# Tap gradients of a depthwise convolution: from TensorE products to GpSimd products and sums

## The chip, the core and the metric

The kernel runs on one core of a Trainium2 chip. The core has TensorE (PE: matrix products; the profile shows its weight loads as PEld), VectorE (DVE), ScalarE (ACT), GpSimd (POOL) and SyncE (SP, which here only starts DMAs). Each engine works through its own list of instructions in order and waits on semaphores for the others. SBUF is the on-chip memory, PSUM the small memory that TensorE writes its products to; GpSimd works on SBUF only in this kernel. The metric is the device time of one execution in microseconds. Times of before and after are medians of several executions; the profile is one further execution with its own time.

## The reference

The kernel computes the output and all gradients of one branchformer block, for x of 2 x 4000 x 144 in bfloat16. What matters here is the gated branch and its convolution over time:

```python
h = _gelu(jnp.einsum('btd,de->bte', xc, w_mlp_in))
u, g = (h[..., :D].copy(), h[..., D:].copy())
g = _layernorm(g, axis=-1)
gp = jnp.pad(g, ((0, 0), (pad, pad), (0, 0)))
gc = jnp.zeros_like(g)
for i in range(K):
    gc = gc + gp[:, i:i + T, :] * dw_csgu[i][None, None, :]
loc = jnp.einsum('btd,de->bte', u * gc, w_mlp_out)
```

The other branch is softmax attention over the 4000 positions. The reference takes the vector-Jacobian product of the whole block. The gradient of the five taps, `dw_csgu` (5 x 144), is for tap i and channel c the sum over batch and time of g(t + i - 2, c) x dgc(t, c), where dgc is the gradient that arrives at gc. Nothing in it couples two channels.

## The kernel before

The two batches are handled one after the other. The 4000 positions of a batch lie as 32 blocks of 125: partition p holds positions 32p to 32p + 31, and block j is the j-th of each partition. So a shift by one position is a shift by one block, and only the ends need a neighbour's partition.

`phase_att` loops over query tiles t = 0 to 32. In a step it forms the scores of tile t and the score gradients of tile t - 1 in four "quads" of products (`quad`, L1028 and L1034) into two PSUM buffers `ps`. VectorE (`S_min` L1052, `PdP` L1070) and ScalarE (L1073) take them out; ScalarE takes exponentials (`P_exp`, L1060); VectorE multiplies in SBUF (L1075). DMA transposes issued by SP turn the results (L1064 for a whole tile, L1255 for half a tile), and TensorE multiplies them again: `Y_half` L1084, `Z_half` L1130, and the gradient of x in `X_group` L1175, which VectorE adds up at L1181. GpSimd scales rows for the X products (L1108 to L1112) and copies remainders into `qz` (L1003), from which SP transposes the next query tile `qt` (L1010).

The gated branch is cut into small functions, `units`, spread over the same loop: 16 rounds per batch, each with two blocks (G2 = 2), about two query tiles per round. `z_unit` to `e_gp` make the forward part of round n, `gc_unit` to `e_dh` the gradient of round o, two rounds behind, `t_unit` transposes. In a ring of five tiles, `gd`, each round leaves its normalized g (index 0) and dgc (index 1); two more such tiles hold the shifted ends.

The tap gradients are made by `dwc_unit`, called after every second round in two parts. Part 0 takes for four blocks and four taps the 128 x 128 matrix of g (shifted) against dgc, summed over positions by TensorE (L668); part 1 takes the fifth tap (L670) and the last 16 channels of all taps (L671). Only the diagonals of these matrices are wanted. `flush` copies each result by ScalarE into the SBUF buffer `l_fl` (L650), and GpSimd adds it to the accumulator `A_dwc` (L651). `dwi_unit` does the same for another weight gradient, with L683, and shares `flush` and `l_fl`. At the end `Final.dwc` picks the diagonals out by six masked products of VectorE (L1677, L1678), transposes them on TensorE and stores `out5` in six DMAs.

The order in which every engine's instructions stand is written out: the table `ORDER` holds, for each engine, the numbers of the instruction groups in the order to be issued, made beforehand by a planner outside the kernel, and `Planner.plan` imposes it. Whenever a group is added or taken away, the whole table has to be made again. WARM is the number of products on zeros that TensorE does at the start, while the first inputs arrive.

Of the kernel before, what the change touches and what calls it, by code (L numbers as in the profile page):

```python
# [15 lines left out]
D = 144  # L16
# [454 lines left out]
WARM = 110  # L471
# [5 lines left out]
def local_units(k, W, b, S, A, es, DHT, ps_w):  # L477
# [5 lines left out]
    sm = es.enter_context(tc.tile_pool(name="loc_sm%d" % b, bufs=4, side="right", reuse_waits="tile"))  # L483
# [20 lines left out]
    fl = pl.tile([128, 512], F32, name="l_fl")  # L504
# [151 lines left out]
    def gnb(h):  # L656
        return gd(h // G2)[:, 0, h % G2, 0:128]

    def dwc_unit(g, part):
        pw = ps_w.tile([128, 512], F32, tag="w")  # L660
        bl = blocks(g)
        for n_, (gg, bi) in enumerate(bl):
            i = G2 * gg + bi
            first, last = n_ == 0, n_ == len(bl) - 1
            t = gd(gg + 1)
            if part == 0:
                for kk in range(4):
                    nc.tensor.matmul(pw[:, kk * 128:(kk + 1) * 128], gnb(i + kk), t[:, 1, bi, 0:128], start=(first and kk == 0), stop=last, skip_group_check=True)  # L668
            else:
                nc.tensor.matmul(pw[:, 0:128], gnb(i + 4), t[:, 1, bi, 0:128], start=first, stop=last, skip_group_check=True)  # L670
                nc.tensor.matmul(pw[0:80, 128:128 + D], rem[:, 0, i:i + 5, :].rearrange("p a b -> p (a b)"), t[:, 1, bi, :], start=False, stop=last, skip_group_check=True)  # L671
        if part == 0:
            flush(pw[:], 128, A.dwc[:, 0:512])
        else:
            flush(pw[:, 0:128], 128, A.dwc[:, 512:640])
            flush(pw[0:80, 128:128 + D], 80, A.dwc[0:80, 640:784])
# [12 lines left out]
    def add(f, *a):  # L689
        def u():  # L690
            f(*a)
        u.tag = f.__name__[:6] + (str(a[-1]) if f.__name__ in ("z_unit", "dwc_unit") else "")
        units.append(u)

    def round_(n, o, c):

        new = [(z_unit, n, 0), (z_unit, n, 1), (e_tanh, n), (e_h, n), (e_stats, n), (dug_unit, n), (e_gn, n), (e_dgc, n), (e_m, n), (e_gp, n)]
        old = [(gc_unit, o), (e_du, o), (dgn_unit, o), (e_dh, o)]
        end = [(dhT_unit, o)]
        if o is not None and o % 2:  # L700
            end += [(dwc_unit, o, 0), (dwc_unit, o, 1), (dwi_unit, o)]
        tr = [(t_unit, c, c - 2 if c is not None and c >= 2 else None)]
        if n is None:
            new = [None] * 10
        if o is None:
            old, end = [None] * 4, [None]
        if c is None:
            tr = [None]
        for u_ in (new[0:3] + old[0:1] + new[3:5] + old[1:2] + new[5:7] + old[2:3] + new[7:9] + old[3:4] + new[9:10] + tr + end):
            if u_ is not None:  # L710
                add(*u_)
# [12 lines left out]
for _s in """  # L724
PE 10 1 1 1 1 1 1 1 1 1 1 1 1 1 1 1 1 1 1 1 1 1 1 1 1 1 167 3 -169 1 1 1 1 1 1 1 1 1 1 162 2 11 -174 1 1 1 1 1 1 1 1 1 1 1 1 1 1 1 1 1 1 179 2 -180 1
# [1316 lines left out]
```

## Time and profile before

| what | us |
|---|---|
| three timed executions | 1278.3, 1276.53, 1277.78 |
| median | 1277.78 |
| the profiled execution, its own time | 1280.24 |
| its span on the core | 1278.4 |
| mean granted TensorE clock | 0.994 |

The span is cut by engine into busy time; a share is of the span. The loop of the first batch fills the span from about 50 to 565 us, that of the second from about 663 to 1183. The stretch between holds the end of the first batch and the start of the second, and the last 95 us the final products. In lists of groups a row gives the line of the kernel, the engine, the operation, what it writes and reads with its shape, how often it stands, its busy time in us, the mean of one in ns, and behind the second bar the idle time of that engine just before it, with what ended it. In the timeline a row gives start and length in us. Durations of TensorE products overlap, because they are pipelined; what one costs in a row of equal ones is the distance between starts.

### The profile page before, as it was taken

What the parts mean: (1) busy time and instruction counts of PE and PEld (TensorE: products, weight loads), DVE (VectorE), ACT (ScalarE), POOL (GpSimd) and SP (SyncE); (2) the same over time, 40 slices, a digit from 0 to 9 for tenths busy, and PEclk for the clock granted to TensorE, in tenths of its full rate; (3) what the DMA queues carried; (4) which work ended last, traced back from release to release, by engine and by line L of the source; (5) the groups of instructions that cost most, each with busy time, mean ns of one, the idle gap of its engine ahead of it and who ended that gap; (6) DMA issues with size and microseconds to landing.
All of it is one profiled execution on the core that took longest, in us unless ns stands there. A gap on an engine that the chain in (4) does not pass through costs nothing.

```text
span 1278.4 us, 38874 instructions
## 1 busy us (share of the span) xinstructions
PE 1251.6 (98%) x15838; PEld 1040.0 (81%) x15838; DVE 1050.6 (82%) x2825; ACT 760.2 (59%) x1232; POOL 477.5 (37%) x971
## 2 busy tenths in 40 slices
PE   8999999999999999999998999999999999999997
PEld 7778888887888888899887788888878788888996
DVE  7699898988888987879768888888889898977765
ACT  4966666656656665545745666665655666555373
POOL 7643443333433443213623434433334333333020
PEclk9999999999999999999999999999999999999999
DMA  3699899798889888885248898888889888899722
GB/s 104 135 165 153 148 147 166 143 158 143 147 158 155 146 157 150 150 191 152 82 99 159 153 160 155 154 156 154 139 159 155 146 154 145 162 148 172 190 60 67
DMA packets 630206, 186.52 MB, mean 146 GB/s; under 512 B 612336, under 2 KB 624971, under 8 KB 630021
## 3 DMA queue, kind: packets, MB, share of 16 engines
q1 hardware_dynamic: 629271, 183.57, 78.9%
q8 instruction: 124, 2.03, 0.6%
q14 instruction: 55, 0.45, 0.1%
q0 software_dynamic: 208, 0.25, 0.1%
q10 hardware_dynamic: 548, 0.21, 0.1%
HBM read 20.82 MB, written 14.22 MB: 27 GB/s over the span
## 4 chain that ended last, share of the span: by engine, by line
PE 87%; DVE 6%; DMA 3%; POOL 1%; ACT 1%; issue 1%; SPq 0%; POOLq 0%; ACTq 0%; DVEq 0%
PE X L1175 21%; PE ps L1028 15%; PE yz L1130 10%; PE yz L1084 9%; PE ps L1034 7%; PE Hps L1458 4%; PE po L1555 3%; PE pc L608 1%; PE pj L991 1%; DVE Pb L1052 1%; DMA SX<-SX 1%; PE pd L556 1%; PE pd L623 1%; PE pw L668 1%; PE pw L683 1%
## 5 line engine op out<-in xcount | busy, mean ns | idle before, releaser
L1052 DVE TENSOR_SCALAR_CACHE_REDUCE Pb<-ps 125x1000 bf16<-125x1000 f32 x256 | 306.0, 1196 | 82.8 <-PE ps L1034 80.1
L1060 ACT ACTIVATE Pb<-Pb,nm 125x1000 bf16<-125x1000 bf16 x256 | 278.7, 1127 | 110.4 <-DVE nm L1054 104.2
L1175 PE MATMUL X<-SX 125*125 125x144 bf16 x2048 | 297.2, 229 | 2.2 <-ACT l_fl L650 0.7
L1175 PE MATMUL X<-SX,Pb 125*125 125x144 bf16 x2048 | 292.7, 226 | 0.0
L1175 PEld LDWEIGHTS <-SX 125*125 125x125 bf16 x2048 | 259.6, 137 | 25.9 <-issue 24.9
L1073 ACT CAST SX<-ps 125x1000 bf16<-125x1000 f32 x189 | 188.1, 995 | 153.4 <-PE ps L1034 151.5
L1028 PE MATMUL ps<-xaT_m,qt 128*125 128x500 bf16 x1024 | 260.8, 375 | 3.8 <-DVE Pb L1052 3.4
L1175 PEld LDWEIGHTS <-Pb 125*125 125x125 bf16 x2048 | 260.5, 137 | 3.2 <-issue 2.5
L1181 DVE TENSOR_TENSOR acc<-X,acc 125x432 f32<-125x432 f32 x372 | 199.9, 548 | 32.0 <-PE X L1175 30.1
L1028 PEld LDWEIGHTS <-qt 128*125 128x125 bf16 x1024 | 122.1, 137 | 44.0 <-issue 5.5
L1130 PE MATMUL yz<-xa_aug,SX 125*125 125x144 bf16 x2048 | 152.4, 229 | 4.2 <-ACT ty L1100 2.8
L1130 PEld LDWEIGHTS <-SX 125*125 125x125 bf16 x2048 | 140.6, 138 | 11.2 <-issue 8.9
L1084 PE MATMUL yz<-xa_aug,SX 125*125 125x145 bf16 x2048 | 146.8, 227 | 0.1
L1084 PEld LDWEIGHTS <-SX 125*125 125x125 bf16 x2048 | 137.1, 137 | 2.0 <-issue 1.6
L1075 DVE TENSOR_TENSOR SX<-SX,Pb 125x1024 bf16<-125x1024 bf16 x189 | 131.2, 698 | 7.3 <-ACT SX L1073 5.6
L1034 PEld LDWEIGHTS <-qt 16*125 16x125 bf16 x1024 | 36.5, 128 | 99.5 <-issue 99.5
L1034 PE MATMUL ps<-XR,qt 16*125 16x500 bf16 x1016 | 111.7, 420 | 0.0
L1070 DVE TENSOR_TENSOR SX<-ps,Pb 125x1000 bf16<-125x1000 f32 x67 | 79.9, 1192 | 8.0 <-ACT SX L1073 5.2
L651 POOL TENSOR_TENSOR A_dwc<-l_fl,A_dwc 128x512 f32<-128x512 f32 (+2 forms) x48 | 36.6, 762 | 82.2 <-ACT l_fl L650 82.2
L633 POOL TENSOR_SCALAR l_w<-gd,nc,c 125x144 f32<-125x144 bf16 x64 | 29.1, 460 | 90.6 <-DVE c L631 81.7
L526 POOL TENSOR_SCALAR l_a<-l_sq 125x576 bf16<-125x576 bf16 x32 | 23.1, 723 | 94.1 <-ACT l_sq L524 93.7
L1110 POOL TENSOR_SCALAR g<-qz,rl 125x144 f32<-125x144 bf16 x62 | 26.1, 421 | 84.0 <-DVE rl L1090 83.7
(479 smaller groups left out, 2327.4 us busy)
## 6 DMA issues: line engine op xcount, KB each, us to landing
go_h<-in_grad_out_dram SPq DMA_DIRECT2D x4, 567.0 KB
Yg<-ug_d SPq DMA_DIRECT2D x4, 567.0 KB
Yn_d<-yn SPq DMA_DIRECT2D x64, 35.2 KB
Zn_d<-qz SPq DMA_DIRECT2D x64, 35.2 KB
ug_d<-ugr SPq DMA_DIRECT2D x32, 70.3 KB
SX<-in_x_dram SPq DMA_DIRECT2D x16, 140.6 KB
out_dram<-Pb SPq DMA_DIRECT2D x16, 140.6 KB
out_dram<-SX SPq DMA_DIRECT2D x16, 140.6 KB
```

Source lines behind the costliest of these rows:

```text
L1028: mm = nc.tensor.matmul(pp[r // 2][:, r % 2, 0:CH], QT[i][:, 3 * h, 0:PB], xaTm[:, c * CH:(c + 1) * CH], start=True, stop=False)
L1034: nc.tensor.matmul(pp[r // 2][:, r % 2, 0:CH], QT[i][rs, 1 + h, 0:PB], xr, start=False, stop=True)
L1052: nc.vector.tensor_scalar(pv(Pbuf, i % NPB, c2), src, -1.0, 3.0e38, op0=ALU.mult, op1=ALU.min, accum_out=NM[i][:, c2:c2 + 1])
L1060: nc.scalar.activation(v, v, ACT.Exp, bias=NM[i][:, 4:5], scale=-1.0)
L1070: nc.vector.tensor_tensor(pv(Sbuf, i % NDB, c2), src, pv(Pbuf, i % NPB, c2), op=ALU.mult)
L1073: nc.scalar.copy(pv(Sbuf, i % NDB, c2), src)
L1075: nc.vector.tensor_tensor(sc, sc, pchunk(i % NPB, c2), op=ALU.mult)
L1084: nc.tensor.matmul(Y, PT[0:PB, j, 0:PB], xaa[:, j, 0:D + 1], start=(j == 0), stop=(j == NB - 1))
L1130: nc.tensor.matmul(Z, ST[0:PB, j, 0:PB], xaa[:, j, 0:D], start=(j == 0), stop=(j == NB - 1))
L1175: nc.tensor.matmul(X[:, jj, :], l, r, start=(n_ == 0), stop=(n_ == len(ops) - 1))
L1181: nc.vector.tensor_tensor(av, X[:, 0:nj, :], av, op=ALU.add)
L1458: nc.tensor.matmul(H[a // 6][0:rows, a // 3 % 2, (a % 3) * D:(a % 3 + 1) * D], lhs, self.src[h][:, 2 + j, :], start=(j == 0 and a % 3 == 0 ...
```

## The change

The tap gradients no longer go through TensorE. `dwc_unit` now runs after every round and gives GpSimd, for each of the round's two blocks, five products of g (shifted by the tap) and dgc, 125 x 144 each, from bfloat16 into a float32 buffer `l_pr` of 125 x 5 x 144, and one sum of that buffer into the accumulator `A_dwc`, now 125 x 5 x 144. The sum over the 125 partitions is left for the end: `Final.dwc` splits the accumulator into a high and a low bfloat16 part on VectorE and multiplies a column of ones with both on TensorE; the result is stored with one DMA. The flush buffer `fl` of `dwi_unit` is now the front of `l_pr`. To make room, the pool `loc_sm` of small tiles has three buffers instead of four. WARM goes from 110 to 116. The order table is made anew for all five engines, with issue times of SP's DMAs that were taken from a trace; `dwi_unit` now stands before `dwc_unit`.

```diff
-WARM = 110
+WARM = 116
...
-    sm = es.enter_context(tc.tile_pool(name="loc_sm%d" % b, bufs=4, side="right", reuse_waits="tile"))
+    sm = es.enter_context(tc.tile_pool(name="loc_sm%d" % b, bufs=3, side="right", reuse_waits="tile"))
...
-    fl = pl.tile([128, 512], F32, name="l_fl")
+    pr = pl.tile([PB, 5, D], F32, name="l_pr")
+    fl = pr[:].rearrange("p a b -> p (a b)")
...
-    def gnb(h):
-        return gd(h // G2)[:, 0, h % G2, 0:128]
-
-    def dwc_unit(g, part):
-        pw = ps_w.tile([128, 512], F32, tag="w")
-        bl = blocks(g)
-        for n_, (gg, bi) in enumerate(bl):
-            i = G2 * gg + bi
-            first, last = n_ == 0, n_ == len(bl) - 1
-            t = gd(gg + 1)
-            if part == 0:
-                for kk in range(4):
-                    nc.tensor.matmul(pw[:, kk * 128:(kk + 1) * 128], gnb(i + kk), t[:, 1, bi, 0:128], start=(first and kk == 0), stop=last, skip_group_check=True)
-            else:
-                nc.tensor.matmul(pw[:, 0:128], gnb(i + 4), t[:, 1, bi, 0:128], start=first, stop=last, skip_group_check=True)
-                nc.tensor.matmul(pw[0:80, 128:128 + D], rem[:, 0, i:i + 5, :].rearrange("p a b -> p (a b)"), t[:, 1, bi, :], start=False, stop=last, skip_group_check=True)
-        if part == 0:
-            flush(pw[:], 128, A.dwc[:, 0:512])
-        else:
-            flush(pw[:, 0:128], 128, A.dwc[:, 512:640])
-            flush(pw[0:80, 128:128 + D], 80, A.dwc[0:80, 640:784])
+    def dwc_unit(g):
+        t = gd(g + 1)[:, 1]
+        for bi in range(G2):
+            for kk in range(5):
+                h = G2 * g + kk + bi
+                nc.gpsimd.tensor_tensor(pr[:, kk, :], gd(h // G2)[:, 0, h % G2, :], t[:, bi, :], op=ALU.mult)
+            nc.gpsimd.tensor_tensor(A.dwc[:], pr[:], A.dwc[:], op=ALU.add)
...
-        if o is not None and o % 2:
-            end += [(dwc_unit, o, 0), (dwc_unit, o, 1), (dwi_unit, o)]
+        if o is not None:
+            if o % 2:
+                end += [(dwi_unit, o)]
+            end += [(dwc_unit, o)]
...
     def dwc(self):
...
+        self.jf = fp.tile([128, D], F32, name="jf")
+        hi, lo = (self.early.tile([PB, 5 * D], BF, name="dwc_%s" % n) for n in ("h", "l"))
+        o5 = self.early.tile([1, 5 * D], BF, name="o5")
+        v = A.dwc[:].rearrange("p a b -> p (a b)")
+        nc.vector.tensor_copy(hi[:], v)
+        nc.vector.tensor_tensor(lo[:], v, hi[:], op=ALU.subtract)
+        one = self.one
+        for q in range(2):
+            c = slice(360 * q, 360 * q + 360)
+            pt = self.pt([1, 360], F32)
+            nc.tensor.matmul(pt[:], one, hi[:, c], start=True, stop=False)
+            nc.tensor.matmul(pt[:], one, lo[:, c], start=False, stop=True)
+            nc.scalar.copy(o5[:, c], pt[:])
+        nc.sync.dma_start(k.out5.rearrange("(o a) b -> o (a b)", o=1), o5[:])
...
-    A.dwc = ap.tile([128, 784], F32, name="A_dwc")
+    A.dwc = ap.tile([PB, 5, D], F32, name="A_dwc")
...
+    F.one = SS[1].xa_aug[:, 0, D:D + 1]
```

The table `ORDER`, replaced as a whole, is left out.

More of the change, by code (lines that the diff above doesn't have):

```diff
@@ L691, in u @@
             f(*a)
-        u.tag = f.__name__[:6] + (str(a[-1]) if f.__name__ in ("z_unit", "dwc_unit") else "")
+        u.tag = f.__name__[:6] + (str(a[-1]) if f.__name__ == "z_unit" else "")
         units.append(u)
@@ L724 @@
 for _s in """
-PE 10 1 1 1 1 1 1 1 1 1 1 1 1 1 1 1 1 1 1 1 1 1 1 1 1 1 167 3 -169 1 1 1 1 1 1 1 1 1 1 162 2 11 -174 1 1 1 1 1 1 1 1 1 1 1 1 1 1 1 1 1 1 179 2 -180 1
[33 rows of a table removed]
-DVE 9 111 23 -135 149 15 2 2 3 -2 1 -5 2 5 12 -5 -6 8 -6 11 -6 -6 2 1 8 -2 40 -2 -39 40 -18 -17 23 -2 4 -6 56 -36 34 -70 -1 -1 3 1 75 -28 -12 -3 41
[47 rows of a table removed]
-Activation 132 -3 -1 5 1 1 -4 -1 76 -3 4 -3 5 13 -9 -2 6 6 109 5 -92 89 -83 85 -84 -28 111 -81 84 -82 4 73 -49 6 1 4 4 -6 18 6 4 18 1 -9 -5 26 1 2 4 1
[24 rows of a table removed]
-Pool 168 -8 9 233 -243 -15 -21 291 -253 -3 245 -238 -3 -41 3 40 -42 24 -21 1 60 -59 18 74 -4 200 -248 -4 38 215 -250 96 -92 88 84 -99 54 4 -19 61 -20
[19 rows of a table removed]
-SP 0 1 135 -134 1 135 286 -420 145 7 -151 1 420 -278 277 -418 130 284 -282 1 10 98 175 -1 -270 1 135 -137 4 132 -133 95 66 -173 172 -167 183 -189 188
[16 rows of a table removed]
+PE 10 1 1 1 1 1 1 1 1 1 1 1 1 1 1 1 1 1 1 180 3 -182 1 1 1 1 1 1 1 1 1 1 175 2 11 -187 1 1 1 1 1 1 1 1 1 1 1 1 1 1 1 1 1 1 1 1 1 189 2 -190 1 1 1 1 1
[33 rows of a table added]
+DVE 9 117 37 -14 -141 170 5 1 -3 -2 6 -3 -2 6 12 -10 12 -13 2 1 1 3 46 -41 -4 42 -1 -39 -4 42 -39 22 -15 19 4 -2 -4 -19 73 1 3 -74 1 48 -47 32 4 -1 40
[47 rows of a table added]
+Activation 141 -6 -1 4 -1 2 73 -3 4 -3 -70 -4 81 11 -9 4 6 -14 36 89 -2 -81 1 -28 107 -77 81 3 -78 79 -83 80 -3 -49 6 1 4 4 -6 18 6 4 16 3 -14 26 1 2
[23 rows of a table added]
+Pool 408 -234 1 -46 38 -1 254 -11 -244 -15 -23 3 -2 3 1 36 -4 -31 288 -229 -19 52 -4 -45 -6 2 -3 38 215 -271 1 116 -4 8 -23 100 -42 -4 -15 -117 154 4
[27 rows of a table added]
+SP 0 1 4 -2 156 -157 2 150 -12 285 -421 137 -136 149 -11 109 -110 286 -270 95 173 1 -276 5 273 -276 7 270 -139 1 -133 160 -1 16 -1 -189 2 9 -10 348 1
[17 rows of a table added]
 """.strip().replace("\n ", " ").split("\n"):
@@ L1671, in dwc @@
         k, nc, A, fp, W = self.k, self.k.nc, self.A, self.fp, self.W
-        dwc_c = fp.tile([128, 5], F32, name="dwc_c")
-        dwc_s = fp.tile([80, 1], F32, name="dwc_s")
-        self.jf = jf = fp.tile([128, D], F32, name="jf")
-        av = A.dwc
-        for kk in range(5):
-            nc.vector.scalar_tensor_tensor(jf[:, 0:128], av[:, kk * 128:(kk + 1) * 128], 1.0, W.ident[:], op0=ALU.mult, op1=ALU.mult, accum_out=dwc_c[:, kk:kk + 1])
-        nc.vector.scalar_tensor_tensor(jf[0:80, 0:DR], av[0:80, 640 + 128:640 + D], 1.0, W.mask[:], op0=ALU.mult, op1=ALU.mult, accum_out=dwc_s[:])
-        dwc_b = fp.tile([128, 5], BF, name="dwc_b")
-        nc.vector.tensor_copy(dwc_b[:], dwc_c[:])
-        dwc_sb = fp.tile([80, 1], BF, name="dwc_sb")
-        nc.vector.tensor_copy(dwc_sb[:], dwc_s[:])
-        pt = self.pt([5, 128], BF)
-        nc.tensor.transpose(pt[:], dwc_b[:], W.ident[:])
-        o5 = fp.tile([5, 128], BF, name="o5")
-        nc.scalar.copy(o5[:], pt[:])
-        nc.sync.dma_start(k.out5[:, 0:128], o5[:])
-        pt = self.pt([1, 80], BF)
-        nc.tensor.transpose(pt[:], dwc_sb[:], W.ident[0:80, 0:80])
-        o5s = fp.tile([1, 5, DR], BF, name="o5s")
-        nc.scalar.copy(o5s[:].rearrange("p a b -> p (a b)"), pt[:])
-        for kk in range(5):
-            nc.sync.dma_start(k.out5[kk:kk + 1, 128:D], o5s[:, kk, :])
+        self.jf = fp.tile([128, D], F32, name="jf")
[12 more added lines that the diff above has]
+        nc.sync.dma_start(k.out5.rearrange("(o a) b -> o (a b)", o=1), o5[:])
     def qk(self):
```

286 rows, old and new, of the table ORDER are left out of this document.

## The prediction

> **What bounds the kernel now.** I read the busy shares first, then the loop over query tiles as two windows, then the groups that the change touches, and last single stretches of the timeline.
>
> The first part of the page and its chain of work:
>
> ```profile
> PE 1251.6 (98%) x15838; PEld 1040.0 (81%) x15838; DVE 1050.6 (82%) x2825; ACT 760.2 (59%) x1232; POOL 477.5 (37%) x971
> ...
> PE 87%; DVE 6%; DMA 3%; POOL 1%; ACT 1%; issue 1%; SPq 0%; POOLq 0%; ACTq 0%; DVEq 0%
> ```
>
> TensorE is busy in all but 26.8 us of the span and carries 87% of the chain. VectorE is second, GpSimd last. The same for the loop of each batch alone (columns: busy us of each engine and its instructions, granted clock, share of the DMA engines, GB/s):
>
> ```profile
> 96.00:544.00 448.00, 444.68 (x5588) 363.81 (x5588) 383.85 (x973) 274.22 (x424) 168.60 (x342) 1.00 0.88 152
> 704.00:1152.00 448.00, 444.88 (x5557) 362.31 (x5555) 382.49 (x973) 271.75 (x417) 163.68 (x339) 1.00 0.88 153
> ```
>
> In 896 us of loop TensorE idles 6.4 us, at a granted clock of 1.00. VectorE is at 85.5%, the DMA engines at 88%, GpSimd at 37%. So TensorE sets the pace and work taken from it should come off the time, but two others lie within 15% of it. Its pipelined durations (219 ns each) are not the price; the distance of starts is. One group of those removed, and what follows it:
>
> ```profile
> 145.43 0.29 PE L668 MATMUL pw<-gd,gd 125*128 125x128 bf16 x2
> ...
> 146.27 0.22 PE L668 MATMUL pw<-gd,gd 125*128 125x128 bf16 x1
> 146.33 0.23 PE L1175 MATMUL X<-SX 125*125 125x144 bf16 x1
> ```
>
> Sixteen products take from 145.43 to 146.33, 0.90 us, 56 ns each, with other work close before and behind. The rows by line and shape that price the GpSimd and VectorE side (busy us, mean ns of one, then idle time before):
>
> ```profile
> L651 POOL TENSOR_TENSOR A_dwc<-l_fl,A_dwc 128x512 f32<-128x512 f32 x16 | 21.0, 1310 | 53.0 <-ACT l_fl L650 53.0
> L651 POOL TENSOR_TENSOR A_dwc<-l_fl,A_dwc 80x144 f32<-80x144 f32 x16 | 8.2, 510 | 14.8 <-ACT l_fl L650 14.8
> L1112 POOL TENSOR_TENSOR SX<-g,g 125x144 bf16<-125x144 f32 x62 | 32.5, 524 | 2.0
> L1075 DVE TENSOR_TENSOR SX<-SX,Pb 125x1024 bf16<-125x1024 bf16 x189 | 131.2, 698 | 7.3 <-ACT SX L1073 5.6 <-ACT Pb L1060 1.7
> ```
>
> And a place where GpSimd and VectorE meet:
>
> ```profile
> 1152.31 1.31 POOL L651 TENSOR_TENSOR A_dwc<-l_fl,A_dwc 128x512 f32<-128x512 f32 x1 [2.46 <-ACT l_fl L650]
> 1152.40 1.53 DVE L640 TENSOR_TENSOR dhr<-l_dd,gpr 125x576 bf16<-125x576 bf16 x1
> ...
> 1153.99 0.58 PE L683 MATMUL pw<-xa_aug,dhr 125*96 125x144 bf16 x6 [0.52 <-DVE dhr L640]
> ```
>
> The VectorE product has a median of 452 ns over 32. Here it starts 0.09 us into a GpSimd sum of two SBUF operands, lasts 1.53 us, and ends 0.31 us after that sum; TensorE then waits 0.5 us for it. This is the one thing in the trace that speaks against the change.
>
> **The change part by part.**
>
> *TensorE, removed.* Per pair of rounds the first part takes 0.90 us (above) and the second, four L670 and four L671 products from 150.37 to 150.84, 0.47 us. Two batches of eight pairs: 16 x 1.37 = 21.9 us. All of it lies in the loop, where TensorE idles 0.7%, so I count the whole: -21.9.
>
> *ScalarE, removed.* 48 copies out of PSUM at L650, 9.3 + 4.2 + 4.3 = 17.8 us. ScalarE idles over a third of the loop; 0. TensorE waited for such a copy only once, 0.7 us. A PSUM buffer of the pool shared by all small products is needed 32 times less; also 0.
>
> *GpSimd, added.* Each of 32 rounds has ten products of 125x144 to float32 and two sums of 125x720. A two-operand row of 144 has a median of 485 to 488 ns (L651 with 80x144, L1112). For 720, the sums of 144 and of 512 have medians of 485 and 1273 ns, 2.14 ns a column, so 1273 + 208 x 2.14 = 1.72 us. A round is 10 x 0.487 + 2 x 1.72 = 8.3 us, 32 of them 266 us; 36.6 us of old sums go. GpSimd comes to 477.5 + 229 = 707 us, 56% of a shorter span. Its idle time in the loop, 564 of 896 us, covers this, so the busy time itself costs 0.
>
> *What stands behind these on GpSimd.* In the new order products stand singly or in runs of up to five among the copies into qz, which the qt transposes and then the score products need, the scaled rows for X, and l_w. A run of five and a sum is 4.2 us. Such an operation waits for what was put before it if its own input is early. In the loop of before no wait of TensorE for GpSimd reaches 0.3 us in sum, so there is distance between these results and their use. From 0 to +10 (one product's 0.49 us in 20 of the 62 tile steps); nearest is the old row, I take +2.
>
> *A wait that is added.* The buffer of the products is also the flush buffer of the second weight gradient. So the copy L650 of a 96x432 tile, 16 times, waits on ScalarE until a GpSimd sum has read the buffer, and three of five products wait for the sum into A_dWiT behind it. On ScalarE the exponentials (L1060) and score casts (L1073) stand behind that copy. Old copies waited for GpSimd in the same way, 14 times, 10.0 us, and TensorE felt 0.7 us of it. New: 0 to 16 x 1.72 = 27 us on ScalarE; at that row's share (0.7 of 10.0) 0 to +2 on TensorE. I take 0.
>
> *Meeting VectorE.* Ten VectorE lines multiply or add two SBUF tensors: L1075 189 times and nine of the gate 32 times each, 477 in all. Their busy time over count times median (131.2 - 189 x 0.683 and so on) is 9.9 us too long in sum, beside 477.5 us of GpSimd. Low: 229 added us at that rate, +5 us on VectorE. High: 477 starts in 1,050 us of loop are one in 2.2 us; 156 us of products would meet 71 of them with 0.24 us left, 110 us of sums 50 with 0.86 us left, 60 us; less 8 for the old sums, 52. Nearest is L651 itself: by the timeline six such starts fall into the 54.6 us of its 64 sums, one in 9 us, a quarter of chance, each drawn out by 0.33 us on average. The 266 us then meet 29, at 0.33 us 10 us. I take 15, because the sums are longer than these: VectorE in the loop goes from 85.5% to 89% of a loop 2% shorter. How much of it TensorE feels is not shown: of the 9.9 us I find the one 0.5 us wait above, 5%; at worst all. With a third less idle time on VectorE than before I take a third, +5, range 0 to +52.
>
> The Trainium skill's "SBUF — State Buffer", section "SBUF: two separate sides", says that GpSimd and a VectorE operation with two SBUF inputs share a port pair as an exclusive lock, and the loser waits for the whole instruction. The 1.53 us row agrees; by that rule the high end, 52 us, is the sum for orders that do not keep the two apart.
>
> *The end.* The tap gradients' last step loses six small VectorE products, two casts and five of six stores, and gains a cast and a difference of 125x720 and four one-row products. By L1181 (432 columns 0.60 us, 144 columns 0.30 us) the two are 0.9 us each, about what six of L1677 and L1678 (0.28 and 0.16 us) took. It stands beside the H products, where TensorE is busy 31.3 of 32 us (1184 to 1216): 0. The last round's 8.3 us on GpSimd has idle time before the halo loads' memsets at 1177 (it idles 8.4 us before 1169.3 alone): 0.
>
> *Head, pool and order.* Six more warm-up products at 0.19 us: +1, or 0 where TensorE idles. Three instead of four buffers for one-column statistics: they turn over once or twice a round of 33 us; 0. The order table is new for all engines. On SP the half-tile transposes (L1255, about 2 us of issue each) stood back to back in 32 pairs, behind which anything else on SP waits 4 us; now 13 pairs are left. What that gives can't be read from the trace: in the loop TensorE has 6.4 us to win back and 20 us outside; what a worse order loses has no bound there, but TensorE's largest single wait for a DMA is 1.3 us. From -5 to +10; I take 0.
>
> Sum against the profiled execution's 1280.24 us: -21.9 + 2 + 5 + 1 = 1266.3. It ran 2.5 us above the median of the three timed runs (1277.78), so 1264 us as a median, 1.1% less.
>
> **The rivals.**
>
> *VectorE is blocked until it sets the pace* (slower). The place is L1075 and the gate's products, in front of the evictions L1052 that give TensorE its two score buffers back. For: the 1.53 us row, and sums of 1.72 us, longer than any GpSimd operation of the loop now. Against: in the old order the meetings were a quarter of chance. At 52 us, two thirds of it felt, the time is 1280.2 - 21.9 + 35 + 3 - 2.5 = 1294 us. It decides once TensorE feels over 19 us.
>
> *The new order itself loses more than the products give*: over 19 us of new waits, 1.2 us in every second tile step of 16.5 us. SP with its in-order transposes is the likeliest place. About 1285 us.
>
> *The gain is hidden* because the DMA engines, 88% busy in the loop, or SP's issue bind where TensorE seems to. TensorE waits for transposes only 1.2 + 1.3 us now, so the time would have to be lost as it shrinks: 1277 us. The Trainium skill's "Perfetto Trace Analysis", section "Identifying the Most-Contended Engine", says that matmul busy time misleads and weight-load busy time is the measure; here that is 81%, which would leave TensorE room and make the cut worth nothing. The row of 56 ns starts without gaps speaks against it.
>
> *The whole gain and some of the idle time*: no meeting felt, the order wins 5 us. 1280.2 - 21.9 - 5 - 2.5 = 1251 us.
>
> **How the numbers follow.** The forecast (1255 to 1274, its bounds by 0 and +14 for what TensorE feels) gets 0.49, the whole gain and more 0.14, hidden 0.08 (about 0.2%, or 2.5 us, is what a measurement of this kernel can tell from no change), blocked VectorE 0.20, the order 0.09. Faster is 0.63, same 0.08, slower 0.29. For 8 in 10 the range goes down to 1254 and up to 1290, leaving out most of the 1251 case and the upper part of the blocked one.
>
> **What would show it.** Right: L668, L670 and L671 gone, TensorE near 1230 us busy and still 97% or more; GpSimd 690 to 740 us; products near 0.49 us and sums near 1.72 us; L1075's mean below 0.8 us; idle time of TensorE in the loop below 15 us. Wrong: L1075 and the gate's products drawn out by more than 40 us in sum with TensorE waiting for L1052 (the lock), or TensorE waiting for transposes, qt or X's scaled rows (the order), or GpSimd's sums beyond 2.2 us.

## The result, and the profile after

The changed kernel takes 1287.27 us (median of 7 runs, 1284.72 to 1293.1), the kernel before 1278.7 (median of 7 runs beside them). The ratio is 1.0072, 95% interval 1.005 to 1.0094: 0.7% slower, where 1.1% faster was forecast. The profiled execution took 1293.1 us, 5.8 above the median, with a span of 1291.3 at a granted clock of 0.993. The line numbers of the loop are three lower than before (L1052 is L1049, L1075 is L1072, L1181 is L1178); L640 is now L641. The new lines are L662, the products, and L663, the sums.

The busy shares and the chain of work of the changed kernel:

```profile
PE 1239.4 (96%) x15462; PEld 1021.4 (79%) x15462; DVE 1093.9 (85%) x2813; ACT 746.6 (58%) x1184; POOL 707.7 (55%) x1307
...
PE 47%; DMA 6%; DVE 6%; issue 1%; ACT 1%; POOL 0%; SPq 0%; ACTq 0%; DVEq 0%; POOLq 0%
```

The chain of work could be followed back only to 493.8 us, so its shares cover 61% of the span, of which TensorE has 47; they are not to be set beside the 87% of before. TensorE is busy 12.2 us less, but the span less its busy time has grown from 26.8 to 51.9 us. VectorE, from which only a little work was taken, is busy 43 us more. The same two stretches of the loop as before (columns: us of the stretch, busy us and instructions of PE, PEld, DVE, ACT and POOL, granted clock, DMA share, GB/s):

```profile
96.00:544.00 448.00, 430.56 (x5280) 348.69 (x5277) 399.34 (x956) 259.72 (x391) 271.30 (x493) 0.99 0.86 148
704.00:1152.00 448.00, 434.15 (x5345) 351.94 (x5344) 396.51 (x962) 266.02 (x399) 266.13 (x482) 1.00 0.88 152
```

TensorE idles 31.3 of 896 us where it idled 6.4, and VectorE goes from 85.5% to 88.8%. The groups by line and shape:

```profile
L1072 DVE TENSOR_TENSOR SX<-SX,Pb 125x1024 bf16<-125x1024 bf16 x189 | 152.5, 811 | 5.4 <-ACT Pb L1057 2.7 <-ACT SX L1070 2.4
L663 POOL TENSOR_TENSOR A_dwc<-l_pr,A_dwc 125x720 f32<-125x720 f32 x64 | 112.3, 1754 | 2.4
L662 POOL TENSOR_TENSOR l_pr<-gd,gd 125x144 f32<-125x144 bf16 x192 | 96.4, 512 | 2.7
L662 POOL TENSOR_TENSOR l_pr<-gd 125x144 f32<-125x144 bf16 x128 | 62.0, 490 | 1.6
L641 DVE TENSOR_TENSOR dhr<-l_dd,gpr 125x576 bf16<-125x576 bf16 x32 | 21.7, 679 | 0.4
```

GpSimd's side is what was forecast. On VectorE, L1072 went from a mean of 698 to 811 ns and L641 from 489 to 679. And what TensorE waited for:

```profile
PE ps L1025 <- DVE Pb L1049: 9.4, 12, 3.2
PE yz L1127 <- DMA SX<-SX: 9.1, 9, 2.2
...
PE yz L1081 <- DMA SX<-Pb: 4.5, 6, 1.3
PE X L1172 <- DVE acc L1178: 3.0, 6, 1.0
```

The first was 3.4 us before, the second 1.2. So two things have come up: VectorE's evictions are late, and so are transposes. The longest wait, in the timeline:

```profile
500.95 0.45 POOL L662 TENSOR_TENSOR l_pr<-gd 125x144 f32<-125x144 bf16 x1
501.01 3.57 DVE L641 TENSOR_TENSOR dhr<-l_dd,gpr 125x576 bf16<-125x576 bf16 x1
501.37 0.45 POOL L662 TENSOR_TENSOR l_pr<-gd,gd 125x144 f32<-125x144 bf16 x1
501.78 0.45 POOL L662 TENSOR_TENSOR l_pr<-gd 125x144 f32<-125x144 bf16 x1
502.18 0.42 POOL L547 COPY ur<-l_hg 125x288 bf16<-125x288 bf16 x1
502.56 1.70 POOL L663 TENSOR_TENSOR A_dwc<-l_pr,A_dwc 125x720 f32<-125x720 f32 x1
504.34 0.55 POOL L662 TENSOR_TENSOR l_pr<-gd 125x144 f32<-125x144 bf16 x1
504.50 1.19 DVE L1049 TENSOR_SCALAR_CACHE_REDUCE Pb<-ps 125x1000 bf16<-125x1000 f32 x1
505.75 0.99 PE L1025 MATMUL ps<-xaT_m,qt 128*125 128x500 bf16 x2 [3.16 <-DVE Pb L1049]
```

A VectorE product with a median of 0.457 us starts 0.06 us into a GpSimd product and lasts 3.57 us: it ends 0.3 us after the fifth GpSimd instruction in a row. The eviction L1049 stands behind it, and TensorE waits 3.16 us for that. In the stretch right behind this wait (columns as above) TensorE's granted clock is 0.50:

```profile
505.60:512.40 6.80, 6.65 (x45) 5.11 (x45) 4.43 (x12) 0.00 (x0) 0.00 (x0) 0.50 0.62 119
```

Over all timed runs the mean granted clock is the same with and without the load (0.995 in the changed kernel and with memsets in place of the load, 0.994 without any load), so the clock does not make the difference between these.

### The profile page after: what moved, and what is told of

Same layout as the page of the kernel before. It is cut to its first block, busy times and chain, and to the rows that moved or that the text cites. A ratio compares the mean times of both kernels' runs of the same rounds, so it can differ in the third digit from the quotient of the medians.

```text
span 1291.3 us, 38380 instructions
## 1 busy us (share of the span) xinstructions
PE 1239.4 (96%) x15462; PEld 1021.4 (79%) x15462; DVE 1093.9 (85%) x2813; ACT 746.6 (58%) x1184; POOL 707.7 (55%) x1307
## 4 chain that ended last, share of the span: by engine, by line
PE 47%; DMA 6%; DVE 6%; issue 1%; ACT 1%; POOL 0%; SPq 0%; ACTq 0%; DVEq 0%; POOLq 0%
PE X L1172 11%; PE ps L1025 7%; PE yz L1081 5%; PE yz L1127 5%; PE Hps L1455 3%; DMA SX<-Pb 3%; PE ps L1031 3%; PE po L1552 3%; DMA SX<-SX 2%; DVE SX L1072 1%; DVE Pb L1049 1%; PE pd L624 1%; PE pz L1530 1%; PE pj L988 1%; PE pm L1378 1%
## 5 line engine op out<-in xcount | busy, mean ns | idle before, releaser
L1049 DVE TENSOR_SCALAR_CACHE_REDUCE Pb<-ps 125x1000 bf16<-125x1000 f32 x256 | 305.7, 1195 | 61.2 <-PE ps L1031 59.5
L1025 PE MATMUL ps<-xaT_m,qt 128*125 128x500 bf16 x1024 | 261.9, 376 | 10.9 <-DVE Pb L1049 9.4
L1178 DVE TENSOR_TENSOR acc<-X,acc 125x432 f32<-125x432 f32 (+1 forms) x372 | 199.9, 548 | 32.0 <-PE X L1172 30.3
L1025 PEld LDWEIGHTS <-qt 128*125 128x125 bf16 x1024 | 122.9, 137 | 52.1 <-issue 13.5
L1127 PE MATMUL yz<-xa_aug,SX 125*125 125x144 bf16 x2048 | 152.3, 229 | 11.6 <-DMA SX<-SX 9.1
L1072 DVE TENSOR_TENSOR SX<-SX,Pb 125x1024 bf16<-125x1024 bf16 x189 | 152.5, 811 | 5.4 <-ACT Pb L1057 2.7
L1127 PEld LDWEIGHTS <-SX 125*125 125x125 bf16 x2048 | 139.6, 138 | 21.7 <-DMA SX<-SX 13.1
L1081 PE MATMUL yz<-xa_aug,SX 125*125 125x145 bf16 x2048 | 145.3, 227 | 5.9 <-DMA SX<-Pb 4.5
L1081 PEld LDWEIGHTS <-SX 125*125 125x125 bf16 x2048 | 136.9, 137 | 8.2 <-DMA SX<-Pb 6.5
L663 POOL TENSOR_TENSOR A_dwc<-l_pr,A_dwc 125x720 f32<-125x720 f32 x64 | 112.3, 1754 | 2.4
L662 POOL TENSOR_TENSOR l_pr<-gd,gd 125x144 f32<-125x144 bf16 x192 | 96.4, 512 | 2.7
L527 POOL TENSOR_SCALAR l_a<-l_sq 125x576 bf16<-125x576 bf16 x32 | 21.9, 684 | 102.4 <-ACT l_sq L525 102.0
L662 POOL TENSOR_TENSOR l_pr<-gd 125x144 f32<-125x144 bf16 x128 | 62.0, 490 | 1.6
```

The lines of the kernel that those rows point to most:

```text
L662: nc.gpsimd.tensor_tensor(pr[:, kk, :], gd(h // G2)[:, 0, h % G2, :], t[:, bi, :], op=ALU.mult)
L663: nc.gpsimd.tensor_tensor(A.dwc[:], pr[:], A.dwc[:], op=ALU.add)
L1025: mm = nc.tensor.matmul(pp[r // 2][:, r % 2, 0:CH], QT[i][:, 3 * h, 0:PB], xaTm[:, c * CH:(c + 1) * CH], start=True, stop=False)
L1049: nc.vector.tensor_scalar(pv(Pbuf, i % NPB, c2), src, -1.0, 3.0e38, op0=ALU.mult, op1=ALU.min, accum_out=NM[i][:, c2:c2 + 1])
L1072: nc.vector.tensor_tensor(sc, sc, pchunk(i % NPB, c2), op=ALU.mult)
L1081: nc.tensor.matmul(Y, PT[0:PB, j, 0:PB], xaa[:, j, 0:D + 1], start=(j == 0), stop=(j == NB - 1))
```

## The experiments

Three theories. *Hold* (the expectations call it the port theory): GpSimd's instructions keep VectorE's products of two SBUF tensors waiting, and TensorE waits for what VectorE has behind them. *Order*: the new order is worse by itself. *Queue*: what stands behind the load on GpSimd comes late. Each ratio is against the kernel before run beside it, on average 1280 us; 0.001 is 1.3 us. "VectorE" is its busy time in the profiled execution.

| kernel | median us | ratio (95%) | VectorE |
|---|---|---|---|
| before | 1278.7 | 1 | 1050.6 |
| before, no taps | 1269.38 | 0.9928 (0.9905 to 0.9951) | 1048.2 |
| new order, no load | 1274.87 | 0.9951 (0.9932 to 0.997) | 1053.2 |
| memsets for load | 1274.96 | 0.9965 (0.9953 to 0.9978) | 1052.7 |
| one-operand load | 1276.25 | 0.9972 (0.9955 to 0.9989) | 1060.8 |
| products only | 1276.85 | 0.9969 (0.9952 to 0.9985) | 1064.5 |
| sums only | 1276.62 | 0.9968 (0.9948 to 0.9988) | 1067.6 |
| half the load | 1278.61 | 0.9987 (0.9972 to 1.0001) | 1070.5 |
| gaps | 1284.2 | 1.0034 (1.0018 to 1.0051) | 1086.5 |
| after | 1287.27 | 1.0072 (1.005 to 1.0094) | 1093.9 |
| split sums | 1295.56 | 1.0123 (1.01 to 1.0147) | 1089.8 |
| spread | 1326.04 | 1.0347 (1.0323 to 1.0371) | 1102.7 |
| old order with load | 1343.16 | 1.0487 (1.046 to 1.0513) | 1085.8 |

**No taps in the old order.** `dwc_unit` of the kernel before does nothing.

```diff
     def dwc_unit(g, part):
-        pw = ps_w.tile([128, 512], F32, tag="w")
...
+        pass
```

> The kernel before, in its own order, without the tap products of TensorE, the copies out of PSUM and the GpSimd sums behind them; the gradient of the gate's depthwise weights is left out. It prices what was taken from TensorE: 16 x 1.37 = 21.9 us, so 1255 to 1259 us if each microsecond of TensorE counts. If something else binds beside TensorE (the transfers or SP), the time stays above 1270 us. With the run that carries no load in the new order it gives the price of the order by itself: equal within 3 us by the port theory, 15 us or more apart by the order theory.

It took 1269.38 us. The ratio gives -9.2 us (-12 to -6), and the two profiled executions differ by 13.4: about half of the 21.9 us. TensorE's busy time is 23.2 us less (1251.6 to 1228.4), so the work is gone; its idle time rose by 9.9. What it waits for in this kernel (L1009 is L1028 of before, L1156 is L1175, L1111 is L1130):

```profile
PE ps L1009 <- DVE Pb L1033: 7.2, 10, 1.4
...
PE yz L1111 <- DMA SX<-SX: 2.1, 5, 0.5
PE X L1156 <- DVE acc L1162: 1.5, 5, 0.4
```

Before, these were 3.4, 1.2 and 0.3. Summed over all its waits, TensorE now waits 19.9 us for VectorE, where before it waited 13.2. So the removed products had been covering waits of other chains.

**The new order without load.** The changed kernel with an empty `dwc_unit` (all of L662 and L663 out, the other places of the order kept).

> The changed kernel, in its own new order, without the ten products and two sums of GpSimd in each round; the gradient of the gate's depthwise weights is left out, all else is computed. Port theory (GpSimd's reads of two SBUF tensors shut VectorE out, and TensorE waits for the late VectorE results): VectorE falls from 1094 to about 1045 us busy, TensorE's idle time from 52 to about 25 us, and the time is the 1278.7 us of before less the 21.9 us that TensorE lost: 1255 to 1262 us. Order theory (the new order itself is worse): TensorE keeps its idle time, with waits for SX and X rows from a DMA as long as now, and the time stays at 1275 us or more. Half and half would be near 1268 us.

1274.87 us. That is the bound which the expectation named for the order, but the expectation counted on the whole 21.9 us, which the run above shows not to come off. The order is not the main cause: the changed kernel is 12.4 us above this. Against the old order without taps it is +0.0023, 2.9 us, with an uncertainty of 4 (the new end and the warm-ups are in it). But TensorE waits for other things here (L1114 is L1127 of after, L1068 is L1081, L1012 is L1025):

```profile
PE yz L1114 <- DMA SX<-SX: 12.4, 15, 2.6
PE yz L1068 <- DMA SX<-Pb: 8.1, 9, 2.0
...
PE ps L1012 <- DMA qt<-qz: 3.2, 6, 1.2
PE ps L1012 <- DVE Pb L1036: 2.6, 7, 0.5
```

24 us of waits for transposes, where the old order without taps has 2.1 us of the first kind. VectorE is hardly waited for. So in the new order it is the transposes that end last once VectorE is on time.

**Memsets in place of the load.** The same places on GpSimd, nothing read.

```diff
-                h = G2 * g + kk + bi
-                nc.gpsimd.tensor_tensor(pr[:, kk, :], gd(h // G2)[:, 0, h % G2, :], t[:, bi, :], op=ALU.mult)
-            nc.gpsimd.tensor_tensor(A.dwc[:], pr[:], A.dwc[:], op=ALU.add)
+                for _ in range(2):
+                    nc.gpsimd.memset(pr[:, kk, :], 0.0)
+            for _ in range(2):
+                nc.gpsimd.memset(A.dwc[:], 0.0)
+            nc.gpsimd.memset(A.dwc[:, 0, :], 0.0)
```

> The changed kernel with each product and each sum of GpSimd replaced by memsets of about the same length in sum, at the same places and with the same buffers; nothing is read from SBUF by them, and the tap gradient is left out. GpSimd stays near 55% busy and what stands behind these instructions on it waits as long. Port theory: VectorE falls back to about 1050 us busy, no two-operand VectorE instruction above 1.6 us, and the time is 1256 to 1264 us. Queue theory (copies into qz, scaled rows and l_w come late because they stand behind the load on GpSimd): the time stays at 1280 us or more with TensorE's idle time near 50 us.

1274.96 us, with GpSimd busy 665.8 us: the time of no load, and VectorE is back at 1052.7 us. The time lies between the two expectations, the lower of which counted on the whole 21.9 us. The queue theory falls for the places of the changed order. The memsets make 234 us where the load makes 271, and they do not wait for the products' inputs; what that is worth on the queue is not parted from the hold. At the place shown above, the same VectorE product now runs beside memsets:

```profile
493.94 1.97 POOL L662 MEMSET l_pr<- 125x144 f32 x9
...
494.54 0.46 DVE L641 TENSOR_TENSOR dhr<-l_dd,gpr 125x576 bf16<-125x576 bf16 x1
```

0.46 us, not 3.57. The Trainium skill's "SBUF — State Buffer", section "SBUF: two separate sides", limits the contention of a VectorE operation with two SBUF inputs to GpSimd operations that read SBUF; this run agrees.

**Products only, sums only.** One of L662 and L663 left out; the sums add the accumulator to itself.

> The changed kernel with GpSimd's products (320 of 0.49 us, 156 us) but without the sums over them (110 us); the tap gradient is so left incomplete. Port theory, by time of reading: 156 of 266 us of the load gives 59% of the loss, about 1258 + 0.59 x 29 = 1275 us. Port theory, by length of what a start meets: products are short, so well under half, 1262 to 1270 us, unless runs of products without a gap act like one long instruction, which puts it back at 1272 to 1280 us. Order theory: 1283 us or more, as before the cut.

> The changed kernel with GpSimd's sums alone: 64 sums of 125x720 float32, the accumulator added to itself, no products before them; the tap gradient is left out. Without load this order takes 1274.9 us, with the products alone 1276.9, with both 1287.3. If the harm goes with the length of one GpSimd instruction, 110 us of sums of 1.7 us cost nearly all of it: 1282 to 1287 us. If it is the run of five products and a sum without a gap that shuts VectorE out, sums alone cost little more than the products alone: 1276 to 1279 us.

1276.85 and 1276.62 us: 0.0018 and 0.0017 over no load, 2.2 us and within the uncertainty, while both together cost 0.0121, 15.5 us. That fits neither the time of reading nor the length of one instruction, and I took it for the runs without a gap.

**Gaps, split sums.** A one-column memset behind each product and sum; or the sum as five of 125x144.

```diff
                 nc.gpsimd.tensor_tensor(pr[:, kk, :], gd(h // G2)[:, 0, h % G2, :], t[:, bi, :], op=ALU.mult)
+                nc.gpsimd.memset(gap[:, kk:kk + 1], 0.0)
             nc.gpsimd.tensor_tensor(A.dwc[:], pr[:], A.dwc[:], op=ALU.add)
+            nc.gpsimd.memset(gap[:, 5:6], 0.0)
```

> The changed kernel, complete, with a memset of one column behind each product and each sum of GpSimd, 384 more instructions that read nothing. If VectorE gets in as soon as a GpSimd instruction that reads nothing stands between two that read two tensors, the longest VectorE instruction falls from 3.6 to about 2 us, VectorE's busy time by 10 to 20 us, and the time from 1287 to 1278 to 1283 us. If a short gap changes nothing, the longest stays above 3 us and the time at 1285 to 1290 us.

> The changed kernel, complete, with each sum of 125x720 cut into five of 125x144 one behind the other (about 5 x 0.49 = 2.4 us in place of 1.7 us). If VectorE has to wait for the end of one instruction only, the wait per meeting falls from up to 1.7 to up to 0.5 us and the time comes down towards that of the products alone, 1278 to 1282 us. If GpSimd keeps VectorE out through a whole run of such instructions, the longer run makes it the same or worse: 1286 to 1296 us.

With gaps 1284.2 us, below after but with the hold unbroken (L642 is the product of L641, L664 and L666 the gaps):

```profile
497.96 3.73 DVE L642 TENSOR_TENSOR dhr<-l_dd,gpr 125x576 bf16<-125x576 bf16 x1
497.97 0.45 POOL L663 TENSOR_TENSOR l_pr<-gd 125x144 f32<-125x144 bf16 x1
498.37 0.09 POOL L664 MEMSET l_gap<- 125x1 f32 x1
498.42 0.45 POOL L663 TENSOR_TENSOR l_pr<-gd,gd 125x144 f32<-125x144 bf16 x1
...
499.68 1.69 POOL L665 TENSOR_TENSOR A_dwc<-l_pr,A_dwc 125x720 f32<-125x720 f32 x1
501.32 0.09 POOL L666 MEMSET l_gap<- 125x1 f32 x1
501.45 0.55 POOL L663 TENSOR_TENSOR l_pr<-gd 125x144 f32<-125x144 bf16 x1
```

Eleven GpSimd instructions overlap it up to the memset behind the sum. The memsets made no break between the products: the second one starts at 498.42, where the first, from 497.97, ends. So this run does not test a break in GpSimd's reading. Split sums took 1295.56 us; the longest L641 rose to 4.95 us and TensorE's longest wait for the eviction to 5.0 us. So here a shorter instruction did not let VectorE in sooner when the next one followed at once.

This is not the common case. In the changed kernel 103 of VectorE's 477 products of two SBUF tensors are drawn out by 0.1 us or more (40 are without load, by GpSimd's other instructions): 93 of them waited through one GpSimd instruction (37.0 us in sum) and ten through two to five (10.7 us). With the sums split, 23 of 109 waited through two or more.

**Spread.** Products and sums placed evenly among GpSimd's other instructions; only GpSimd's list in the order table differs.

> The changed kernel, complete, with the same products and sums and the order of every other engine untouched, but GpSimd's load spread evenly among its other instructions within each round: 244 of the 384 stand alone and 100 in pairs, where the changed order has 93 alone and 29 pairs and the rest in runs of 3 to 12. If the runs are what shuts VectorE out, its longest instruction falls below 2.5 us, its busy time from 1094 to 1070 to 1080 us, and the time from 1287 to 1277 to 1281 us, at or under the kernel before. If the time of reading as such does the harm, however it is cut up, VectorE stays near 1090 us and the time at 1284 to 1290 us.

1326.04 us, far above both expectations, and VectorE at 1102.7: my theory of the runs as the cause of the whole loss fell. Counted in the trace, 96 of VectorE's 477 products of two SBUF tensors start inside a load instruction here, 100 in the changed kernel: spreading breaks runs and meets as many. And GpSimd's own results come late now, which the changed order had avoided (lines one higher than in the changed kernel):

```profile
PE X L1173 <- POOL SX L1110: 6.2, 6, 1.9
...
PE pt L595 <- POOL gd_rem L569: 2.2, 2, 1.2
```

Over all waits, TensorE waits 11.8 us for GpSimd (2.2 in the changed kernel) and VectorE 45.3 (27.5). TensorE's mean granted clock over the runs is 0.989 against 0.995, by an estimate from these clocks 8 of the 39 us. How the rest is shared between queue and hold no run shows: memsets were not put at these places.

**Old order with the load.** The kernel before without taps, with the load beside the same GpSimd neighbours as in the changed kernel, on a scratch tile.

```diff
...
+                nc.gpsimd.tensor_tensor(av[:, kk, :], sc[:, 0, :], sc[:, 0, :], op=ALU.mult)
+            nc.gpsimd.tensor_tensor(av, av, av, op=ALU.add)
```

> The kernel before without its taps, in its old order, with GpSimd's new load put among the same GpSimd neighbours as in the changed kernel: ten products and two sums a round with the same shapes and types, on a scratch tile and the accumulator, so that nothing waits for them and they wait for nothing; the tap gradient is left out. Without load this order takes 1269.4 us. If the load costs the same in any order, 1269.4 + 12.4 = 1280 to 1283 us, no gain over before. If the new order makes the load dear (it has no slack for a late VectorE), it stays at 1270 to 1276 us.

1343.16 us, far outside both expectations. VectorE is held no more than in the changed kernel (1085.8), but the rows that GpSimd makes for X come late (lines six lower than before):

```profile
PE ps L1022 <- DVE Pb L1046: 15.6, 20, 1.9
PE X L1169 <- POOL SX L1106: 14.8, 7, 5.5
```

TensorE waits 22.3 us for GpSimd in all (2.8 without load) and VectorE 46.4 (24.2). The mean granted clock is 0.984 against 0.996, by an estimate 16 of the 74 us. So the old order does not carry this load, and the remade one does; that it is the queueing which the remade order makes free is argued from these waits and from the memsets in the remade order, since the old order was not run with memsets.

**Less work on VectorE.** L1075 (L1072) on 512 of 1024 columns, in three kernels.

```diff
-                nc.vector.tensor_tensor(sc, sc, pchunk(i % NPB, c2), op=ALU.mult)
+                nc.vector.tensor_tensor(sc[:, 0:512], sc[:, 0:512], pchunk(i % NPB, c2)[:, 0:512], op=ALU.mult)
```

> The kernel before without its taps (which took 1269.4 us where the sum gave 1257), and VectorE's product of the score gradient with the probabilities over 512 of 1024 columns only: the other half is not multiplied and the tap gradient is left out. That takes 189 x about 0.32 = 60 us from VectorE and leaves TensorE and the transfers as they are. If the missing 10 us are TensorE waiting for VectorE, the time comes down to 1257 to 1262 us. If they are the transfers or SP, it stays within 3 us of 1269.

> The changed kernel with the same VectorE product over 512 of 1024 columns; the other half is not multiplied. The load on GpSimd stays. If the 12 us of the load are VectorE's delay passed on to TensorE, 60 us less work on VectorE pays for the 47 us that it is held up, and the time falls to the floor of this order without load, 1275 us, or below: 1268 to 1277 us. If the load harms by another way (results of GpSimd that come late), it stays above 1282 us.

> The control: the kernel before with the same VectorE product over 512 of 1024 columns, taps kept. TensorE waited for VectorE's evictions for 3.4 us in the loop before, so if TensorE sets the pace this gives 2 to 5 us, about 1275 to 1278 us. More than 10 us would mean that VectorE bound the kernel before already.

VectorE's busy time fell by 46 to 49 us in each. The control took 1277.18 us (ratio 0.9973, 0.996 to 0.9985: -3.5 us), no taps 1264.96 (0.9872, 0.9852 to 0.9891), after 1283.29 (1.002, 1.0003 to 1.0036). For the last two that is 7 us less than without the cut by the ratios, with 4 of uncertainty, and 4 us by the medians. So the amount of VectorE's work sets the time of neither; 46 us less of it do not pay for 41 us of hold. In the changed kernel so cut L641 still lasts up to 3.57 us. Its time is where the expectation put a harm by late results of GpSimd, against which the memsets speak; that single late instructions of VectorE do the harm is argued, not tested.

**One operand, half the load.**

```diff
...
+                nc.gpsimd.tensor_scalar(pr[:, kk, :], t[:, bi, :], 0.5, 0.25, op0=ALU.mult, op1=ALU.add)
+            nc.gpsimd.tensor_scalar(A.dwc[:], pr[:], 0.5, 0.25, op0=ALU.mult, op1=ALU.add)
```

> The changed kernel with each product and each sum of GpSimd replaced by an instruction on the same columns, types and place that reads one tensor and two constants (times 0.5, plus 0.25); the tap gradient is left out. If it is the reading of two SBUF tensors that holds VectorE up, VectorE falls to 1050 to 1060 us busy and the time to 1275 to 1278 us, as with the memsets. If any reading of SBUF by GpSimd does it, VectorE stays at 1085 to 1095 us and the time at 1283 to 1289 us.

> The changed kernel with the load of one of the two tiles of each round: five products and a sum in place of ten and two, 133 of 266 us of GpSimd, in the same order; half of the tap gradient is left out. Without load 1274.9 us, with all of it 1287.3. If each microsecond of hold counts alike, half the load gives 1281 us. If the first 15 us or so of VectorE's lateness are covered by TensorE's waits for transposes, as products alone and sums alone (14 and 17 us later on VectorE, 2 us on the time) suggest, it gives 1275 to 1278.5 us.

The one-operand load is shorter too (160 us in all, not 271):

```profile
L661 POOL TENSOR_SCALAR l_pr<-gd 125x144 f32<-125x144 bf16 x320 | 106.2, 348 | 4.5
L662 POOL TENSOR_SCALAR A_dwc<-l_pr 125x720 f32<-125x720 f32 x64 | 53.5, 836 | 2.5
```

It lengthens VectorE by 7.6 us and costs 0.0021, within the uncertainty. Reading one tensor holds too, more weakly: 24 of the 1024-column products start inside one and take 826 ns on average, with 303 ns of the GpSimd instruction left, against 44 with 1134 ns and 549 left in the changed kernel (the median of those that meet none of the load is 684 and 683).

Half the load took 1278.61 us, between the two expectations. Set beside the others, by VectorE's busy time over that of no load: 11.3 us (products) cost 2.3, 14.4 (sums) 2.2, 17.3 (half) 4.6, 33.3 (gaps) 10.6, 40.7 (all) 15.5. The first 14 us cost 0.15 each, the next 26 0.5 each; each cost is uncertain by 3 to 4 us. Split sums do not lie on this line: 36.6 us on VectorE cost 22.0, so the sum of the hold alone does not give the time. With no load TensorE waits 20.5 us for the transposes of SX, with all of it 13.6: VectorE's lateness first takes the place of waits that are there anyway. TensorE's waits for VectorE, over all, go the other way, from 12.8 to 27.7 us. That is argued from these waits; no run took the transposes' lateness away.

## Why the prediction was wrong

Two steps failed: that the whole of TensorE's 21.9 us would come off the time, and the count of VectorE's meetings with GpSimd, taken at a quarter of chance. By the prediction's own steps, with the runs that price each:

| step | forecast | measured |
|---|---|---|
| TensorE, removed | -21.9 | -9.2 (no taps) |
| new order, warm-ups and end | +1 (-5 to +10) | +2.9, uncertain by 4 |
| queueing on GpSimd | +2 | +1.8, uncertain by 3 (memsets) |
| meeting VectorE, in us of VectorE | 15 | 40.7 |
| what TensorE feels of it | +5 | +13.7 (after less memsets) |
| sum | -14 | +9.2 |

Each measured time is a difference between neighbours in a row of runs from before to after, so that column adds up by itself; -9.2 and +13.7 are each uncertain by 3.

*TensorE, removed.* The 16 x 1.37 us were right: 23.2 us of busy time went. What failed was "I count the whole". That TensorE idles only 6.4 us in the loop shows that it has work, not that nothing else would be late without it; about half did not come off, and TensorE's idle time rose by 9.9 us, 6.7 of it in waits for VectorE. That is half of the rival "the gain is hidden", though mostly not by transfers: the trace shows waits for VectorE's evictions, for its sums of X and for transposes, each small. 46 us less work on VectorE took 7 us off without the taps, uncertain by 4, but 3.5 with them too, so it did not bring the rest back. What would is open.

*Meeting VectorE.* This term failed most. Its mechanism and its place (L1075 and the gate's products ahead of L1052) were right; the count was not. The third that TensorE feels came out too (13.7 of 40.7), but by luck: it was taken from VectorE's idle time, and the runs show no fixed share, 0.15 for the first 14 us and 0.5 for the next 26. I took a quarter of chance, 29 meetings, from six starts in 54.6 us of L651. Counted after: 100 meetings at 0.36 us each, 36 us. 477 starts in 1,050 us are one in 2.2 us; the 270 us of load met one in 2.7 us, near chance. The old sums stood where VectorE seldom had such a product, and a sample of six says nothing of twelve instructions a round put elsewhere. The high end of 52 us, which the rule of the Trainium skill ("SBUF — State Buffer", the same section) gives, was the better value. Of the 103 products drawn out, 93 waited for the end of one instruction, as that rule has it; for the other ten the measured wait was longer than the rule says.

Neither error alone turns the sign: with 9.2 for 21.9 the sum is -1, with 13.7 for 5 it is -5. So the rival "VectorE is blocked until it sets the pace" named the cause, but VectorE's work did not set the pace (46 us less of it took off 7), and the 19 us from which it was to decide were not reached. It needed the lost half of the gain as well.

*The rest.* GpSimd came to 707.7 us busy (forecast 707), sums to a median of 1712 ns (1720), products to 456 (487). The copies of the flush into `l_pr` did not wait for GpSimd at all (L651's 4.2 us of idle time before it are for PE). The order's price is in the range given; its trace shows the sign named for it, waits for transposes, 12.4 us at L1127 without load where before had 1.2. The time is within the range of 1254 to 1290 us; the direction is not the one given 0.63. Of the signs named, L1072's mean of 811 ns is beyond the 0.8 us given for "right", TensorE's 31.3 us of idle time in the loop beyond the 15, and the sign for "wrong" appeared: L1072 and the gate's products drawn out by 48 us in sum (9.9 before), TensorE waiting for L1049. The halved clock behind the longest wait stands in no term.

## What to carry to other kernels

In a kernel like this one, price work that moves to GpSimd by the VectorE instructions of two SBUF tensors that will start inside it, at chance level unless the order keeps them apart, and not by GpSimd's idle time; memsets at the same places show in one run about how much of the loss is the hold and how much the queue. Price work that leaves a busy engine by a run that only leaves it out: here about half of it did not come off, though the engine was busy 98% of the time. And the place of such a load in the order counts: the same load at evenly spread places, or a like one in the old order, cost three to five times as much as in the order made for it.

## What the runs showed of the hardware

- Of the 103 VectorE products of two SBUF tensors that were drawn out by 0.1 us or more in the changed kernel, 93 waited through one GpSimd instruction; some waited through several in a row: five, 3.57 us in place of 0.46. All five that passed three or more ended behind a break of 0.08 us or longer in GpSimd's instructions. In the lines shown, the product behind the sum starts 0.08 us after it ends, while those ahead each start before the one in front ends. With one-column memsets (0.09 us) the products still followed one another without a break, and one VectorE product took 3.73 us through eleven instructions. Whether a break alone would let VectorE in was not tested, and why most got in after one instruction no run shows.
- GpSimd memsets hold nothing up: 234 us of them left VectorE at 1052.7 us, as without load (1053.2).
- VectorE's evictions L1049, which read PSUM, are not held: 55 that start inside the load take 1193 ns on average, the 148 that meet none of it 1196. Nor are the statistics L542, which read one SBUF tensor: 22 take 296 ns, as do the 41 that meet none.
- Right behind the 3.16 us wait TensorE's granted clock was 0.50 for 6.8 us. The runs that lose most have the lowest mean clock: 0.989 spread and 0.984 in the old order with load, against 0.995.
